# Splitting one of the two whole block products of a second channel matmul, with the residual moved into accumulating DMAs and the first load cut in quarters

## The chip, the cores and the metric

One core of a Trainium2 chip. The metric is the device time of one execution in microseconds (us). Profiles are single executions taken by the hardware profiler; their span is mostly 1.7 to 1.9 us shorter than the device time of the same execution. Ratios are computed as the mean time of one kernel's runs over that of the other kernel's runs of the same rounds, so they are not quite the ratio of the medians that are quoted.

## The reference, cut to what matters

```python
# attention with a hash mask, then an MLP mixer:
# x: (4, 768, 512), w_ch1: (512, 1536), w_ch2: (1536, 512), all fp32
u = x + h.transpose(0, 2, 1)                 # token mixing
h2 = np.maximum(u @ w_ch1, 0.0) @ w_ch2      # channel mixing: two matmuls
return (u + h2).astype(np.float32)           # "+ u" is the residual
```

The change touches the second channel matmul, the residual, and the first load of the attention.

## The kernel before: the parts that matter

Tokens are handled in three stages of 1024. In each, both channel matmuls are done by a Strassen-like scheme with seven block products instead of eight. In the second matmul five of the seven products, p2, p3, p5, p6 and p7, are themselves made of seven smaller ones (`product`); p1 and p4 are made whole (`whole_product`).

```python
def whole_product(s, j, name):               # 2 x 6 matmuls of 128x512
    ...
    for m in range(KC):
        accumulate(split(pair[:, m])[:, ns], lambda k: w[:, k, P*m:P*m+P],
                   lambda k: right[:, ns, k], range(HC))
    fetch_left(7 * s + j + 2)                # weights of the product after next

def product(s, j, name, q, between):         # 7 x 3 matmuls of 128x256
    part(0, 4, b00); part(1, 5, b10); ...    # small products into PSUM blocks
    for work in between: work()              # VectorE work of other blocks
    qs[:, 0] = ps[1] + p1; ...               # (VectorE) combine into q
    begin(ORDER[j + 1])                      # operand sums of the next product

ps = whole_product(s, 0, "p1")
...
product(s, 3, "p3", q3, [add(q57, q7, q5), residual(q57, 1, 1), residual(q7, 1, 0)])
product(s, 4, "p6", q6, [add(q3, q3, q5), residual(q3, 0, 1)])
product(s, 5, "p2", q2, [add(q6, q6, q1), add(q57, q57, q6), store(q57, 1, 1),
                         add(q3, q3, q6), store(q3, 0, 1), add(q7, q7, q6), residual(q1, 0, 0)])
ps = whole_product(s, 6, "p4")
add(q2, q2, q1)(); store(q2, 0, 0)()
for m in range(KC): ...                      # q7 += ps[m]; store in pieces
```

`residual` is a VectorE add of 128x1024; `store` a DMA of 512 KB from the SyncE queue. At the start, the first q and k come in two halves (each with both q and k), one on the SyncE and one on the ScalarE queue, while 14 dummy matmuls keep TensorE busy.

Of the kernel before, what the change touches and what calls it, by code (L numbers as in the profile page):

```python
# [48 lines left out]
def kernel(  # L49
# [214 lines left out]
    def attention(pool, psum, W1, W2, x0):  # L264
# [3 lines left out]
        def load_qk(n):  # L268
            if n >= len(pairs):
                return  # L270
            b, hp = pairs[n]
            t = pool.tile([P, 2, S], F32, name="qk", tag="qk", bufs=3)
            for sl in [slice(0, HALF), slice(HALF, S)] if n == 0 else [slice(0, S)]:
                issuer = nc.scalar if n == 0 and sl.start else nc.sync
                issuer.dma_start(out=t[:, :, sl], in_=qk[b, hp, :, :, sl])
            loaded[n] = [t, None, None, None]
# [171 lines left out]
        for _ in range(14):  # L448
            nc.tensor.matmul(idle[:D, :D], ones, ones, start=True, stop=True)
# [226 lines left out]
    def channels(pool, psum, SW1, second, TA, judge):  # L676
# [30 lines left out]
        def split(a):  # L707
            return a.rearrange("p (n t) -> p n t", n=2)

        def hidden(s, t):  # L710
# [18 lines left out]
            if s:  # L729
                look()  # L730
# [14 lines left out]
        ORDER = ["p1", "p5", "p7", "p3", "p6", "p2", "p4"]  # L745
        WHOLE = ["p1", "p4"]
# [3 lines left out]
        def prepare():  # L750
# [34 lines left out]
            return [[*sums, whole("p1"), whole("p4"), parts("p7")], *([parts(p)] for p in ["p3", "p6", "p5", "p2"])]  # L785
# [44 lines left out]
        def combine(to, a, op, b):  # L830
            for h in range(2):
                for n in range(2):
                    nc.vector.tensor_tensor(operand[to][h][n], operand[a][h][n], operand[b][h][n], op=op)

        def whole_product(s, j, name):
            pair = blocks()[2]
            if "WC2" in second:
                w = second.pop("WC2")[:, :HC, : DM // 2]
            else:
                w = left_at(7 * s + j)[:, : HC * 2 * P].rearrange("p (k c) -> p k c", k=HC)  # L840
            right = R[int(RIGHT[name][1])]
            for m in range(KC):
                final = s == last and name == ORDER[-1] and m == KC - 1
                for ns in [slice(0, 1), slice(1, 2)] if final else [slice(0, 2)]:
                    accumulate(
                        split(pair[:, m])[:, ns], lambda k: w[:, k, P * m : P * m + P],
                        lambda k: right[:, ns, k], range(HC),
                    )
            fetch_left(7 * s + j + 2)
            return pair  # L850

        def product(s, j, name, q, between):
# [26 lines left out]
            qs = q.rearrange("p i (n t) -> p (i n) t", n=2)  # L879
            nc.vector.tensor_tensor(qs[:, 0], ps[1], p1, op=ALU.add)  # L880
            nc.vector.tensor_tensor(p57[:, 0], p57[:, 0], p57[:, 1], op=ALU.add)
            if j + 1 < 6:
                begin(ORDER[j + 1])
# [5 lines left out]
        def outputs(s):  # L889
# [5 lines left out]
            def residual(to, i, n):  # L895
                return add(to, to, XT[:, KC * i : KC * i + KC, sl[n]])

            def store(q, i, n):
                return lambda: nc.sync.dma_start(
                    out=out[KC * i : KC * i + KC, :, sl[n]].rearrange("m p t -> p m t"), in_=q,  # L900
                )

            ps = whole_product(s, 0, "p1")
            combine("x", "r3", ALU.subtract, "r1")
            begin("p5")
            nc.scalar.copy(q1, ps)
            q7, q57, q3, q5 = [output_at(i) for i in range(4)]
            q6 = q2 = q5
            product(s, 1, "p5", q5, [lambda: combine("r0", "x", ALU.subtract, "r0")])
            product(s, 2, "p7", q7, [lambda: combine("r1", "r2", ALU.subtract, "x")])  # L910
            product(s, 3, "p3", q3, [add(q57, q7, q5), residual(q57, 1, 1), residual(q7, 1, 0)])
            product(s, 4, "p6", q6, [add(q3, q3, q5), residual(q3, 0, 1)])
            product(s, 5, "p2", q2, [
                add(q6, q6, q1), add(q57, q57, q6), store(q57, 1, 1), add(q3, q3, q6), store(q3, 0, 1),
                add(q7, q7, q6), residual(q1, 0, 0),
            ])
            ps = whole_product(s, 6, "p4")
            add(q2, q2, q1)()
            store(q2, 0, 0)()
            if s < last:  # L920
                inputs(s + 1, T, 0)
                inputs(s + 1, T, 1)
            for m in range(KC):
                final = s == last and m == KC - 1
                for cols in [slice(0, TT // 2), slice(TT // 2, TT)] if final else [slice(0, TT)]:
                    nc.vector.tensor_tensor(q7[:, m, cols], ps[:, m, cols], q7[:, m, cols], op=ALU.add)  # L926
                    issuer = nc.scalar if final and cols.start else nc.sync
                    at = slice(sl[0].start + cols.start, sl[0].start + cols.stop)
                    issuer.dma_start(out=out[KC + m, :, at], in_=q7[:, m, cols])
# [34 lines left out]
        for s in range(last + 1):  # L964
            for t in range(HC):
                if s == 0 and (t == 5 if judge else t == 0):
# [7 lines left out]
                else:  # L974
# [16 lines left out]
    def with_token_weights(stage):  # L991
        with tc.tile_pool(name="tok", bufs=1, reuse_waits="tile") as tok:
# [10 lines left out]
            f"p{i}": dram.tile([P, (4 if i in (1, 4) else 7) * n], F32, name=f"left{i}") for i in range(1, 8)  # L1003
# [95 lines left out]
```

## Time and profile before

| | |
|---|---|
| median of 4 runs, beside the changed kernel | 829.11 us (827.83 to 829.17) |
| medians of 9 to 11 runs in the three later sessions | 827.39 to 827.60 us |
| span of the profile | 825.5 us |
| TensorE busy | 816.4 us, 99% |
| VectorE busy | 630.3 us, 76% |
| the three channel stages, first to last matmul | 414.40 us |
| last matmul to end of span | 6.78 us |

Read a page from the engine shares and the chain that ended last: the chain tells which work set the end. Here it is one row of matmuls from the first load to the last store, so a change must be judged by what it does to TensorE's work, to the few microseconds before its first useful matmul and after its last, and to whether it is ever made to wait.

### The profile page before, as it was taken

To read this page: it belongs to the slowest core of one execution; us is meant where nothing else is said; L and a number is where in the kernel's file an instruction comes from. 1 tells how busy PE (TensorE), PEld (TensorE's weight loads), DVE (VectorE), ACT (ScalarE), POOL (GpSimd) and SP (SyncE) were. 2 spreads that over 40 slices of the span, in tenths; PEclk is the share of its full clock that TensorE was granted. 3 is DMA by queue.
4 is the path that set the end of the run, shared out by engine and by line. 5 is a ranking of instruction groups with operands and counts; after the bars stand their busy time and mean duration, and the time that the engine had idled before them with its cause. 6 is when DMAs were issued, how large, how long until landed. Compare 5 with 4: busy or idle time off the path is not lost.

```text
span 825.5 us, 9922 instructions
## 1 busy us (share of the span) xinstructions
PE 816.4 (99%) x3719; PEld 436.1 (53%) x3719; DVE 630.3 (76%) x831; ACT 326.0 (39%) x516; POOL 26.1 (3%) x37
## 2 busy tenths in 40 slices
PE   8999999999999999999999999999999999999996
PEld 4444444444444444455544468744447864444884
DVE  4889898989988667798486579956669984635993
ACT  5777788888887774211011211111111102121110
POOL 1000000000000000000011100001010001010000
PEclk9999999999999999999999999999999999999999
DMA  4335354546424226562014444453434345100432
GB/s 159 138 141 173 134 155 135 167 159 201 141 93 118 80 79 182 188 204 76 0 51 150 132 174 143 153 189 114 138 130 171 134 128 194 38 1 0 164 143 106
DMA packets 59784, 106.84 MB, mean 129 GB/s; under 512 B 28296, under 2 KB 37328, under 8 KB 57808
## 3 DMA queue, kind: packets, MB, share of 16 engines
q1 hardware_dynamic: 59168, 105.52, 38.7%
q8 instruction: 31, 0.51, 0.2%
q10 hardware_dynamic: 560, 0.61, 0.2%
q14 instruction: 25, 0.20, 0.1%
HBM read 84.43 MB, written 21.04 MB: 128 GB/s over the span
## 4 chain that ended last, share of the span: by engine, by line
PE 98%; DMA 0%; DVE 0%; ACT 0%; issue 0%; ACTq 0%
PE b L697 50%; PE sc L340 19%; PE acc L387 16%; PE t L618 5%; PE t L637 5%; PE sums L411 2%; PE hp L301 1%; DMA qk<-in_qk 0%; PE hw L319 0%; DVE second L926 0%; ACT vt L292 0%; ACT e L347 0%; ACT g L306 0%; DVE g L305 0%; DVE bits L321 0%
## 5 line engine op out<-in xcount | busy, mean ns | idle before, releaser
L704 ACT COPY p<-b 128x512 f32<-128x512 f32 (+1 forms) x84 | 44.3, 549 | 296.0 <-PE b L697 296.0
L340 PE MATMUL sc<-qk 64*128 64x384 f32 x768 | 158.5, 492 | 0.3 <-ACT e L347 0.3
L347 ACT ACTIVATE e<-sc 128x768 f32<-128x768 f32 x192 | 153.1, 812 | 13.4 <-PE sc L340 12.5
L697 PE MATMUL b<-R,second 128*128 128x256 f32 (+1 forms) x588 | 158.0, 427 | 0.0
L697 PEld LDWEIGHTS b<-R,second 128*128 128x128 f32 x588 | 111.7, 190 | 43.8 <-issue 32.0
L387 PE MATMUL acc<-e,vn 128*64 128x384 f32 x768 | 130.9, 490 | 0.0
L379 DVE TENSOR_TENSOR esd<-esd,e 128x768 f32<-128x768 f32 x128 | 122.3, 955 | 10.4 <-ACT e L347 0.5
L340 PEld LDWEIGHTS sc<-qk 64*128 64x128 f32 x768 | 66.5, 187 | 55.6 <-issue 45.1
L387 PEld LDWEIGHTS acc<-e,vn 128*64 128x64 f32 x768 | 52.3, 137 | 74.9 <-issue 74.3
L697 PE MATMUL b<-XT,WC 128*128 128x512 f32 x144 | 64.7, 592 | 0.0
L340 PE MATMUL sc<-bits 64*128 64x384 bf16 x384 | 62.9, 323 | 0.2 <-DVE bits L323 0.2
L731 POOL TENSOR_TENSOR p<-p,p 128x512 f32<-128x512 f32 x18 | 22.8, 1268 | 723.1 <-ACT p L704 723.1
L697 PEld LDWEIGHTS b<-XT,WC 128*128 128x128 f32 x144 | 27.3, 190 | 34.1 <-issue 33.6
L939 DVE TENSOR_REDUCE largest<-seen 128x1 f32<-128x1536 f32 x16 | 28.0, 1751 | 22.3 <-DMA seen<-in_qk 22.1
L618 PE MATMUL t<-x,W 128*128 128x512 f32 x96 | 41.8, 593 | 0.0
L736 DVE TENSOR_TENSOR R<-p,u 128x512 f32<-128x512 f32 x18 | 12.4, 687 | 38.5 <-POOL p L731 38.5
L637 PE MATMUL t<-W,r 128*128 128x384 f32 x128 | 41.8, 486 | 0.0
L736 DVE TENSOR_TENSOR R<-b,u 128x512 f32<-128x512 f32 x36 | 23.2, 686 | 24.1 <-PE b L697 24.1
L432 ACT COPY rec<-rec 32x384 f32<-32x384 f32 x64 | 32.6, 509 | 12.9 <-DVE rec L426 12.4
L375 DVE SCALAR_TENSOR_TENSOR esd<-e 128x768 f32<-128x768 f32 x32 | 30.5, 954 | 9.3 <-ACT e L347 9.3
L393 ACT ACTIVATE num<-acc,vsum 128x384 f32<-128x384 f32 x32 | 18.6, 581 | 41.6 <-PE acc L387 41.2
L697 PE MATMUL b<-TA,WC 128*128 128x512 f32 x72 | 33.8, 592 | 0.0
(116 smaller groups left out, 922.3 us busy)
## 6 DMA issues: line engine op xcount, KB each, us to landing
second<-left SPq DMA_DIRECT2D x15, 1344.0 KB
raw<-in_moe_w_ch SPq DMA_DIRECT2D x16, 768.0 KB
seen<-in_qk SPq DMA_DIRECT2D x16, 768.0 KB
qk<-in_qk SPq DMA_DIRECT2D x15, 768.0 KB
vn<-in_v SPq DMA_DIRECT2D x16, 384.0 KB
vt<-in_vT SPq DMA_DIRECT2D x16, 384.0 KB
bounced<-stage SPq DMA_DIRECT2D x32, 192.0 KB
x<-bounced SPq DMA_DIRECT2D x4, 1536.0 KB
```

What stands on the lines that cost most here:

```text
L340: nc.tensor.matmul(sc[:, i, :HALF], t[rows, 1, P * c : P * c + P], t[rows, 0, qs], start=start, stop=not start,)
L347: nc.scalar.activation(e, sc[:, :, :HALF], ACT.Exp, scale=SCALE)
L375: nc.vector.scalar_tensor_tensor(self.d, es[0], NR * EPS, es[1], op0=ALU.add, op1=ALU.add,)
L379: nc.vector.tensor_tensor(self.d, self.d, e, op=ALU.add)
L387: nc.tensor.matmul(acc[D * i : D * i + D], vn[:, i, c], e[:, i], start=(c == 0), stop=(c == NR - 1),)
L432: nc.scalar.copy(rec[other : other + 32, h], rec[at : at + 32, h])
L618: nc.tensor.matmul(ps, W1[:, r, P * j : P * j + P], x[:, r], start=(r == 0), stop=(r == NR - 1),)
L637: nc.tensor.matmul(ps[:, :HALF], r1[:, j, P * cb : P * cb + P], W2[:, j, HALF * half : HALF * half + HALF], start=(j == 0), stop=(j == NJ ...
L697: nc.tensor.matmul(ps, left(k), right(k), start=start and k == ks[0], stop=stop and k == ks[-1], skip_group_check=True,)
L704: nc.scalar.copy(c if shape is None else shape(c), ps)
L736: nc.vector.tensor_tensor(r[k], split(a), split(u), op=ALU.add)
L939: nc.vector.tensor_reduce(largest[:, n : n + 1], t, AX.XY, ALU.max, apply_absolute_value=True,)
```

## The change

The intent: p4 is split like the others, which saves an eighth of its matmul columns. To make room on VectorE, the residual adds go: the residual (XT) is written to the output early in each stage, and each finished block is added to it by an accumulating DMA, one per product. p6 and p3 trade places. The sums of weight blocks that a split needs come two per step instead of one. In the last stage q7 keeps its residual on VectorE and is stored plainly, in four pieces. The first load comes in two quarters and a half, with 16 dummy matmuls.

```diff
-            for sl in [slice(0, HALF), slice(HALF, S)] if n == 0 else [slice(0, S)]:
-                issuer = nc.scalar if n == 0 and sl.start else nc.sync
-                issuer.dma_start(out=t[:, :, sl], in_=qk[b, hp, :, :, sl])
+            if n:
+                nc.sync.dma_start(out=t, in_=qk[b, hp])
+            else:
+                for i in range(2):
+                    nc.sync.dma_start(out=t[:, i, :HALF], in_=qk[b, hp, :, i, :HALF])
+                nc.scalar.dma_start(out=t[:, :, HALF:], in_=qk[b, hp, :, :, HALF:])
...
-        for _ in range(14):
+        for _ in range(16):
...
-        ORDER = ["p1", "p5", "p7", "p3", "p6", "p2", "p4"]
-        WHOLE = ["p1", "p4"]
+        ORDER = ["p1", "p5", "p7", "p6", "p3", "p2", "p4"]
+        WHOLE = ["p1"]
...
             def store(q, i, n):
-                return lambda: nc.sync.dma_start(
-                    out=out[KC * i : KC * i + KC, :, sl[n]].rearrange("m p t -> p m t"), in_=q,
-                )
+                def job():
+                    nc.gpsimd.dma_start(
+                        out=out[KC * i : KC * i + KC, :, sl[n]].rearrange("m p t -> p m t"), in_=q,
+                        accum_op=ALU.add,
+                    )
+                return job
...
+            product(s, 3, "p6", q6, [add(q57, q7, q5)])
+            q3, q2, q4 = q6, q5, q57
+            product(s, 4, "p3", q3, [
+                add(q6, q6, q1), add(q57, q57, q6), store(q57, 1, 1), add(q5, q5, q6), add(q7, q7, q6),
             ])
-            ps = whole_product(s, 6, "p4")
+            end = [add(q3, q3, q5), store(q3, 0, 1)]
             if s < last:
+                product(s, 5, "p2", q2, end)
+                product(s, 6, "p4", q4, [
+                    add(q2, q2, q1), store(q2, 0, 0), lambda: inputs(s + 1, T, 0), lambda: inputs(s + 1, T, 1),
+                ])
+                add(q4, q4, q7)()
+                store(q4, 1, 0)()
+            else:
+                product(s, 5, "p2", q2, [*end, add(q7, q7, XT[:, KC:, sl[0]])])
+                product(s, 6, "p4", q7, [add(q2, q2, q1), store(q2, 0, 0)], ...)   # stores q7 plainly
...
+        def residual(s):                       # before the second step of each stage
+            ...  nc.sync.dma_start(out=out[...], in_=XT[...])
```

More of the change, by code (lines that the diff above doesn't have):

```diff
@@ L728, in hidden @@
             nc.vector.tensor_scalar(r[0], r[0], 0.0, None, op0=ALU.max)
-            if s:
+            if jobs:
+                for job in jobs.pop(0):
+                    job()
+            elif s:
                 look()
@@ L784, in prepare @@
             sums = weight_sums(WC2, SW2, slice(0, HC), slice(HC, NHT), low, high)
-            return [[*sums, whole("p1"), whole("p4"), parts("p7")], *([parts(p)] for p in ["p3", "p6", "p5", "p2"])]
+            return [
+                sums, [whole("p1"), parts("p7")], [parts("p6")], [parts("p3")], [parts("p5")], [parts("p2")],
+                [parts("p4")],
+            ]
         def place(i):
@@ L828, in begin, with combine @@
             nc.vector.tensor_tensor(b01, b01, b00, op=ALU.subtract)
-        def combine(to, a, op, b):
-            for h in range(2):
-                for n in range(2):
-                    nc.vector.tensor_tensor(operand[to][h][n], operand[a][h][n], operand[b][h][n], op=op)
+        def combine(to, a, op, b, where=[(0, 0), (0, 1), (1, 0), (1, 1)]):
+            for h, n in where:
+                nc.vector.tensor_tensor(operand[to][h][n], operand[a][h][n], operand[b][h][n], op=op)
         def whole_product(s, j, name):
@@ L842, in whole_product, with product @@
             for m in range(KC):
-                final = s == last and name == ORDER[-1] and m == KC - 1
-                for ns in [slice(0, 1), slice(1, 2)] if final else [slice(0, 2)]:
-                    accumulate(
-                        split(pair[:, m])[:, ns], lambda k: w[:, k, P * m : P * m + P],
-                        lambda k: right[:, ns, k], range(HC),
-                    )
+                accumulate(
+                    split(pair[:, m]), lambda k: w[:, k, P * m : P * m + P], lambda k: right[:, :, k], range(HC),
+                )
             fetch_left(7 * s + j + 2)
             return pair
-        def product(s, j, name, q, between):
+        def product(s, j, name, q, between, final=None):
             half = slice(0, TT // 2)
@@ L879, in product @@
             qs = q.rearrange("p i (n t) -> p (i n) t", n=2)
+            if final:
+                nc.vector.tensor_tensor(p1, p1, qs[:, 0], op=ALU.add)
             nc.vector.tensor_tensor(qs[:, 0], ps[1], p1, op=ALU.add)
+            if final:
+                nc.sync.dma_start(out=final(0, 0), in_=qs[:, 0])
             nc.vector.tensor_tensor(p57[:, 0], p57[:, 0], p57[:, 1], op=ALU.add)
-            if j + 1 < 6:
+            if final:
+                nc.vector.tensor_tensor(qs[:, 3], qs[:, 3], u, op=ALU.add)
+                nc.vector.tensor_tensor(qs[:, 3], qs[:, 3], p57[:, 0], op=ALU.add)
+                nc.sync.dma_start(out=final(1, 1), in_=qs[:, 3])
+                for i in (1, 2):
+                    nc.vector.tensor_tensor(qs[:, i], qs[:, i], u, op=ALU.add)
+                for i, a in [(1, ps[2]), (2, ps[3])]:
+                    nc.vector.tensor_tensor(qs[:, i], a, qs[:, i], op=ALU.add)
+                    (nc.scalar if i == 2 else nc.sync).dma_start(out=final(i // 2, i % 2), in_=qs[:, i])
+                return
+            if j < 6:
                 begin(ORDER[j + 1])
@@ L893, in add @@
                 return lambda: nc.vector.tensor_tensor(to, a, b, op=ALU.add)
-            def residual(to, i, n):
-                return add(to, to, XT[:, KC * i : KC * i + KC, sl[n]])
             def store(q, i, n):
-                return lambda: nc.sync.dma_start(
-                    out=out[KC * i : KC * i + KC, :, sl[n]].rearrange("m p t -> p m t"), in_=q,
-                )
+                def job():
+                    nc.gpsimd.dma_start(
+                        out=out[KC * i : KC * i + KC, :, sl[n]].rearrange("m p t -> p m t"), in_=q,
+                        accum_op=ALU.add,
+                    )
@@ L903, in outputs @@
+                return job
             ps = whole_product(s, 0, "p1")
-            combine("x", "r3", ALU.subtract, "r1")
+            combine("x", "r3", ALU.subtract, "r1", [(0, 1)])
             begin("p5")
+            combine("x", "r3", ALU.subtract, "r1", [(0, 0), (1, 0), (1, 1)])
             nc.scalar.copy(q1, ps)
-            q7, q57, q3, q5 = [output_at(i) for i in range(4)]
-            q6 = q2 = q5
+            q7, q57, q6, q5 = [output_at(i) for i in range(4)]
             product(s, 1, "p5", q5, [lambda: combine("r0", "x", ALU.subtract, "r0")])
@@ L910, in outputs @@
             product(s, 2, "p7", q7, [lambda: combine("r1", "r2", ALU.subtract, "x")])
-            product(s, 3, "p3", q3, [add(q57, q7, q5), residual(q57, 1, 1), residual(q7, 1, 0)])
-            product(s, 4, "p6", q6, [add(q3, q3, q5), residual(q3, 0, 1)])
-            product(s, 5, "p2", q2, [
-                add(q6, q6, q1), add(q57, q57, q6), store(q57, 1, 1), add(q3, q3, q6), store(q3, 0, 1),
-                add(q7, q7, q6), residual(q1, 0, 0),
-            ])
-            ps = whole_product(s, 6, "p4")
@@ L918, in outputs @@
-            add(q2, q2, q1)()
-            store(q2, 0, 0)()
+            product(s, 3, "p6", q6, [add(q57, q7, q5)])
+            q3, q2, q4 = q6, q5, q57
+            product(s, 4, "p3", q3, [
+                add(q6, q6, q1), add(q57, q57, q6), store(q57, 1, 1), add(q5, q5, q6), add(q7, q7, q6),
+            ])
+            end = [add(q3, q3, q5), store(q3, 0, 1)]
             if s < last:
-                inputs(s + 1, T, 0)
-                inputs(s + 1, T, 1)
-            for m in range(KC):
-                final = s == last and m == KC - 1
-                for cols in [slice(0, TT // 2), slice(TT // 2, TT)] if final else [slice(0, TT)]:
-                    nc.vector.tensor_tensor(q7[:, m, cols], ps[:, m, cols], q7[:, m, cols], op=ALU.add)
-                    issuer = nc.scalar if final and cols.start else nc.sync
-                    at = slice(sl[0].start + cols.start, sl[0].start + cols.stop)
-                    issuer.dma_start(out=out[KC + m, :, at], in_=q7[:, m, cols])
+                product(s, 5, "p2", q2, end)
[6 more added lines that the diff above has]
+                product(s, 5, "p2", q2, [*end, add(q7, q7, XT[:, KC:, sl[0]])])
+                product(s, 6, "p4", q7, [
+                    add(q2, q2, q1), store(q2, 0, 0),
+                ], lambda i, n: out[KC + i, :, sl[0].start + TT // 2 * n : sl[0].start + TT // 2 * (n + 1)])
@@ L932, in channels @@
+        def residual(s):
+            for i in range(2):
+                for n in range(2):
+                    if s < last or (i, n) != (1, 0):
+                        sl = slice(TT * (2 * s + n), TT * (2 * s + n) + TT)
+                        nc.sync.dma_start(
+                            out=out[KC * i : KC * i + KC, :, sl].rearrange("m p t -> p m t"),
+                            in_=XT[:, KC * i : KC * i + KC, sl],
+                        )
         unseen = list(range(len(pairs))) if judge else []
@@ L965, in channels @@
             for t in range(HC):
+                if t == 1:
+                    residual(s)
                 if s == 0 and (t == 5 if judge else t == 0):
@@ L973, in channels @@
                         job()
-                else:
+                elif (s, t) != (1, HC - 1):
                     look()
@@ L1002 @@
         "passed": {
-            f"p{i}": dram.tile([P, (4 if i in (1, 4) else 7) * n], F32, name=f"left{i}") for i in range(1, 8)
+            f"p{i}": dram.tile([P, (4 if i == 1 else 7) * n], F32, name=f"left{i}") for i in range(1, 8)
         }
```

## The prediction

> **What bounds the kernel now.** I read the page first (engine shares and the chain that ended last), then the TensorE timeline of the last stage, then that of VectorE, then the DMA share microsecond by microsecond.
>
> ```profile
> PE 816.4 (99%) x3719; PEld 436.1 (53%) x3719; DVE 630.3 (76%) x831; ACT 326.0 (39%) x516; POOL 26.1 (3%) x37
> ...
> PE 98%; DMA 0%; DVE 0%; ACT 0%; issue 0%; ACTq 0%
> ```
>
> TensorE (PE) works for 816.4 of 825.5 us and is 98% of the chain that ended last. So there are only three ways to save time: give PE less work, start it earlier, or shorten what follows its last matmul. PE must also never be made to wait. The work touched is the second channel matmul, done three times (once per stage of 1024 tokens) as seven block products p1 to p7. Before, p1 and p4 are made whole, the other five from seven smaller products each. The PE timeline of the last stage (start, duration, instructions):
>
> ```profile
> 752.58 14.35 PE L697 MATMUL b<-R,second 128*128 128x512 f32 x42
> 766.76 1.46 PE L697 MATMUL b<-second 128*128 128x256 f32 x6
> 768.05 7.93 PE L697 MATMUL b<-R,second 128*128 128x256 f32 x36
> 775.83 1.46 PE L697 MATMUL b<-second,second 128*128 128x256 f32 x6
> 777.12 7.93 PE L697 MATMUL b<-R,second 128*128 128x256 f32 x36
> 784.89 1.46 PE L697 MATMUL b<-second 128*128 128x256 f32 x6
> ...
> 799.13 4.05 PE L697 MATMUL b<-R,second 128*128 128x256 f32 x18
> 803.02 1.46 PE L697 MATMUL b<-second 128*128 128x256 f32 x6
> 804.32 14.38 PE L697 MATMUL b<-R,second 128*128 128x256 f32 x54
> ```
>
> An fp32 matmul appears as two instructions. A split product is 7 x 3 matmuls of 256 columns, 42 instructions. The marks 766.76, 775.83 and 784.89 (the fourth small product of three products in a row) lie 9.07 us apart: one split product takes **9.07 us**, 216 ns per instruction. A whole product is 12 matmuls of 512 columns, 24 instructions. The last p4 begins seven groups of 1.296 us after 799.13, at 808.2, and PE ends at 818.7; p1 runs from 752.58 to 762.9 (766.76 less three such groups). So it takes **10.3 us**, 429 ns per instruction.
>
> After the last matmul (VectorE and the issue queues):
>
> ```profile
> 818.73 1.35 DVE L926 TENSOR_TENSOR second<-b,second 128x512 f32<-128x512 f32 x3 [6.98 <-PE b L697]
> 819.45 0.96 SPq L929 DMA_DIRECT2D out<-second  x2
> 820.12 0.37 ACTq L929 DMA_DIRECT2D out<-second  x1
> ```
>
> VectorE sat idle for 6.98 us and only then did three adds: although half of p4's PSUM was finished 5 us before, its add waited for the last matmul. Then 512 KB leave at once. The DMA share shows data moving from 820.25 to about 822.1; the span ends 3.4 us after that.
>
> **What the Trainium skill says.** (1) "TensorE: Matmul & The Clock Gate", section "Wait — 56ns, not 53.3ns?": start to start is N / 2.4 GHz plus about 2.5 ns once warm. The trace has 429 and 216 ns per instruction for 512 and 256 columns, twice what that gives (431 and 218), with a granted clock of 1.00; the ratio is 1.99, so halving the width costs nothing visible. (2) "DMA: Bandwidth & Descriptors", section "SWDGE vs HWDGE vs iDMA": accumulation during a DMA is done only by DMAs issued from GpSimd. The kernel before has none, so no row shows their cost. (3) Same page, "Anatomy of one DMA — SWDGE (gpsimd) path": about 2.0 us plus bytes / 436e3; for 512 KB that is 3.2 us for a plain copy. (4) Same page, "Rules for kernel authors": an accumulating DMA reads its destination and writes it later, so it must wait for the earlier DMA. The early residual write and the later addition are therefore ordered by a semaphore; the trace before cannot show that wait.
>
> **The change part by part.**
>
> *p4 split.* Removed per stage: 24 x 429 ns = 10.30 us of PE; added: 42 x 216 ns = 9.07 us. The gain is 1.23 us a stage, **3.7 us** for three, all on the path, if PE stays fed. Weight loads do not take over: 42 x 190 ns = 8.0 us, beside 9.07.
>
> *VectorE.* Removed per stage: four residual adds of 1.22 us (three in the last stage) and p4's two 0.69 us adds, 6.3 us. Added: p4's operand sums (4 x 0.95), its four combinations (3 x 0.42 + 0.69) and the addition of q7 (1.22), 7.0 us. So the total hardly moves (+0.7 us), but its place does. The tightest spot by program order is p3, now fifth: two operand sums, four adds (4.9 us), two small adds, then the two sums that p2's operand needs. Placing them by durations before, relative to p3's start: operand sums done at 3.7 us, adds at 8.6, small adds at 9.2, p2's operands at 11.2. PE wants p2's third group at 9.07 + 2.59 = 11.66. That leaves a half microsecond of slack: I expect no stall or one of a few tenths.
>
> *DMA.* These rows of the windows (stretch, its length, busy time of PE, weight loads, VectorE, ScalarE and GpSimd, granted clock, then DMA share and GB/s) show what a weight fetch costs:
>
> ```profile
> 772.00:773.00 1.00, 1.00 (x6) 0.89 (x5) 1.00 (x3) 0.00 (x0) 0.00 (x0) 1.00 0.00 0
> 773.00:774.00 1.00, 1.00 (x6) 0.88 (x5) 1.00 (x2) 0.37 (x1) 0.00 (x0) 1.00 1.06 226
> 774.00:775.00 1.00, 1.00 (x7) 0.87 (x6) 0.70 (x2) 0.00 (x0) 0.00 (x0) 1.00 0.99 409
> 775.00:776.00 1.00, 1.00 (x6) 0.90 (x5) 1.00 (x2) 0.00 (x0) 0.00 (x0) 1.00 0.99 419
> 776.00:777.00 1.00, 1.00 (x6) 0.87 (x6) 1.00 (x2) 0.00 (x0) 0.00 (x0) 1.00 0.77 323
> ```
>
> Issued when a product's matmuls end (771.9), 1344 KB are there by about 777; the product that needs them starts at 781.0. p4's fetch grows from 768 to 1344 KB, like the others. An accumulating store of 512 KB moves at most 1 MB through HBM, an estimate of 2.6 us at 400 GB/s, less than those 4 us of slack. The early residual is 2 MB a stage, about 5 us at that rate, in the matmul phase, where the queue is half idle. Its worst effect is in the first stage: six weight-sum jobs now come two per step of 12.05 us, share one buffer, and queue behind the 2 MB. I estimate that VectorE falls behind by some 7 us there, but PSUM and the copies are buffered two steps deep, so PE should not stop.
>
> *Start.* PE's first useful matmul starts at 4.92 us, 0.81 us after the warm-up matmuls end, waiting for the first 384 KB, which travel interleaved with 384 KB from the other queue. A first part half as large is there after some 470 of 780 KB, which at the rates of the first microseconds (about 390 GB/s by then) is some 0.7 us earlier; with two more warm-up matmuls (0.11 us each) ending at 4.3, I count **0.5 us**.
>
> *Tail.* Now the last adds are two of 256 columns (0.77 us instead of 1.38, if both wait for the last matmul), and 256 KB instead of 512 are stored at the end: 0.8 us from issue to first data as before, about 0.6 us instead of 1.6 moving. PE end to last data: 2.2 instead of 3.35 us, **1.1 us** gained.
>
> Sum: 3.7 + 0.5 + 1.1 = 5.3 us. I subtract an expected 0.5 us for small stalls and for the chance that the accumulation ends last: 829.1 - 4.8 = **824.3 us**, 0.6% less.
>
> **Rivals.**
> (a) *The last accumulating store sets the end.* It is issued after q2 is complete, about 5.3 us into p4, and must land within 9.07 - 5.3 + 2.2 = 6.0 us to be hidden. The skill's 3.2 us plus a second read fits; an accumulate at half rate with slow descriptor making on GpSimd does not. One in three; it would cost 1 to 4 us, giving 825 to 828.
> (b) *VectorE becomes the bound inside the products.* For: it is 90 to 100% busy in those windows and p3's slack is half a microsecond. Against: the operand sums come a product ahead. A stall of 0.3 to 1 us in each stage would give 825 to 827.
> (c) *DMA backlog stalls PE in the first stage*, through the shared weight-sum buffer behind the residual. For: two sums a step, against one before. Against: rates near 400 GB/s, and some 5 us of margin even when VectorE is 7 us late. If it happened, 2 to 6 us lost, giving 826 to 830.
> (d) *Accumulating DMAs are much slower than assumed* and delay the weight fetches of every stage: several us each, 830 to 845. Unlikely, 4%.
>
> **Range and chances.** Without any stall 823.8, a little below that if the tail is better; with (a) or (b) up to 828. So 822.0 to 827.8. Two per cent is 16.6 us: no gain here adds up to that, and a loss needs (d) in every stage. Faster by over 2%: 0.01; within: 0.96; slower: 0.03.
>
> **What would show it.** The PE timeline should show p4 as groups of 128x256 and the stage's seven products taking 10.3 + 6 x 9.07 us. PE idle inside the stages should stay under 1 us; idle laid to VectorE in p2 would be (b), to DMA (d), in the first stage's steps (c). The first useful matmul should start at about 4.4 us. After the last matmul there should be two 256-column adds and data for about 2.2 us; if DMA data run on longer, or the chain ends in the GpSimd queue's store, it is (a). The prediction is wrong if PE's idle time grows by more than about 4 us anywhere.

## The result, and the profile after

The changed kernel took 824.48 us (median of 4 runs, 823.69 to 825.05) beside 829.11 us for the kernel before: 4.6 us less; the ratio of the means is 0.9947 (95% interval 0.993 to 0.9964). 824.3 us had been predicted. Two later sessions on other chips gave 824.10 beside 827.55 us (ratio 0.9955) and 824.32 beside 827.60 us (0.9953), which is 3.3 to 3.9 us by one measure or the other. The changed kernel is where it was predicted; the kernel before had in the first session mostly runs of its slower sort, to which I come back.

The TensorE timeline of the changed kernel's last stage (start, duration, engine and line, operation, tiles, shape, instructions):

```profile
751.45 14.35 PE L700 MATMUL b<-R,second 128*128 128x512 f32 x42
765.64 1.46 PE L700 MATMUL b<-second 128*128 128x256 f32 x6
...
801.90 1.46 PE L700 MATMUL b<-second 128*128 128x256 f32 x6
803.19 7.93 PE L700 MATMUL b<-R,second 128*128 128x256 f32 x36
810.96 1.46 PE L700 MATMUL b<-second,second 128*128 128x256 f32 x6
812.26 4.05 PE L700 MATMUL b<-R,second 128*128 128x256 f32 x18
```

The last product now has 256-column groups, and the marks 801.90 and 810.96 show p2 and p4 at a distance of 9.06 us. The chain that ended last shows the same over all stages. Before, its two pieces of channel matmuls (start, duration) are:

```profile
404.48 336.13 PE b L697 x992
740.61 0.11 PE b L955
740.72 77.99 PE b L697 x298
```

and after:

```profile
405.82 333.66 PE b L700 x1028
739.49 0.11 PE b L990
739.60 76.72 PE b L700 x304
```

Each is unbroken: 414.23 against 410.49 us, so **3.74 us** less. But the second starts 1.34 us later than the first: in this pair of profiles the start lost time. The TensorE timeline of the start, before (in brackets the idle time just before and what ended it):

```profile
4.92 1.53 PE L319 MATMUL hw<-qk,projs 128*128 128x384 f32 x4 [0.81 <-DMA qk<-in_qk]
...
9.01 0.91 PE L319 MATMUL hw<-qk,projs 128*128 128x384 f32 x2
```

and of the changed kernel:

```profile
4.61 2.46 PE L322 MATMUL hw<-qk,projs 128*128 128x384 f32 x4
7.00 2.21 PE L343 MATMUL sc<-qk 64*128 64x384 f32 x12
9.04 0.65 PE L343 MATMUL sc<-bits 64*128 64x384 bf16 x6
10.35 0.91 PE L322 MATMUL hw<-qk,projs 128*128 128x384 f32 x2 [0.66 <-DMA qk<-in_qk]
```

The first useful matmul is earlier, 4.61 instead of 4.92 us, but the same four instructions take 2.46 us instead of 1.53, and at 10.35 us TensorE had waited for the other half of the load. The trace's record of the granted clock explains the first: full clock from 6.45 us on, against 3.83 us in the profile of before.

The end, on all engines:

```profile
812.37 1.21 POOL L921 DMA_DIRECT2D out<-second  x1 [6.66 <-DVE p L889]
...
816.34 0.76 DVE L901 TENSOR_TENSOR second<-b,second 128x256 f32<-128x256 f32 x2 [0.59 <-PE b L700]
816.79 0.33 SPq L902 DMA_DIRECT2D out<-second  x1
817.13 0.37 ACTq L902 DMA_DIRECT2D out<-second  x1
```

Two adds of 256 columns after the last matmul, as predicted. But GpSimd issued the last accumulating store at 812.37 us, and the DMA view gives such stores (last number: median us from issue to landing)

```profile
out<-second POOLq DMA_DIRECT2D x11, 512.0 KB, 6.0
```

so it was still under way beside the final plain stores: its last data moved at 818.2 us, and it landed at 818.6. The last data of the final stores themselves moved 3.7 us after the last matmul, against 3.3 us in the profile of before and 2.2 us in the prediction. From the last matmul (816.32) to the end of the span (822.92) are 6.60 us, only 0.2 less than before.

### The profile page after: what moved, and what is told of

Read it like the earlier page. It is cut to its first block, busy times and chain, and to the rows that moved or that the text cites. A ratio compares the mean times of both kernels' runs of the same rounds, so it can differ in the third digit from the quotient of the medians.

```text
span 822.9 us, 10100 instructions
## 1 busy us (share of the span) xinstructions
PE 814.2 (99%) x3765; PEld 445.1 (54%) x3765; DVE 637.8 (78%) x848; ACT 330.0 (40%) x525; POOL 39.8 (5%) x48
## 4 chain that ended last, share of the span: by engine, by line
PE 97%; DMA 1%; ACT 0%; DVE 0%; issue 0%; ACTq 0%
PE b L700 50%; PE sc L343 19%; PE acc L390 16%; PE t L621 5%; PE t L640 5%; PE sums L414 2%; PE hp L304 1%; DMA qk<-in_qk 1%; PE hw L322 0%; ACT vt L295 0%; ACT e L350 0%; ACT g L309 0%; DVE g L308 0%; DVE bits L324 0%; DVE second L901 0%
## 5 line engine op out<-in xcount | busy, mean ns | idle before, releaser
L707 ACT COPY p<-b 128x512 f32<-128x512 f32 (+1 forms) x90 | 47.2, 545 | 296.7 <-PE b L700 292.1
L700 PE MATMUL b<-R,second 128*128 128x256 f32 (+1 forms) x612 | 150.9, 404 | 0.0
L700 PEld LDWEIGHTS b<-R,second 128*128 128x128 f32 x612 | 116.3, 190 | 32.5 <-issue 18.4
L640 PEld LDWEIGHTS t<-W,r 128*128 128x128 f32 x128 | 24.3, 190 | 17.6 <-issue 1.4
```

The lines of the kernel that those rows point to most:

```text
L640: nc.tensor.matmul(ps[:, :HALF], r1[:, j, P * cb : P * cb + P], W2[:, j, HALF * half : HALF * half + HALF], start=(j == 0), stop=(j == NJ ...
L700: nc.tensor.matmul(ps, left(k), right(k), start=start and k == ks[0], stop=stop and k == ks[-1], skip_group_check=True,)
L707: nc.scalar.copy(c if shape is None else shape(c), ps)
```

## The experiments

Twelve kernels ran in three sessions, each on another chip, with five rounds each and the kernel before in the same rounds. All gave correct results. For each, the profile was cut at three places: the first channel matmul, the last matmul, and the end of the span. "Full clock" is the time, from the span's start, at which the trace first records the granted TensorE clock at 1 (the expectation of `again` counts these times 0.25 us later: 6.70 and 4.08).

| kernel | full clock, us | channel starts, us | channel length, us | last matmul to end, us | span, us | median, us | before, same rounds |
|---|---|---|---|---|---|---|---|
| before | 3.83 | 404.31 | 414.40 | 6.78 | 825.49 | 829.11 | |
| changed | 6.45 | 405.66 | 410.66 | 6.60 | 822.92 | 824.48 | 829.11 |
| again (the same) | 3.87 | 403.96 | 410.65 | 6.38 | 820.99 | 824.10 | 827.55 |
| again2 (the same) | 5.82 | 405.72 | 410.66 | 6.61 | 822.99 | 824.32 | 827.60 |
| s1 (changed, old start) | 10.24 | 407.00 | 410.66 | 6.66 | 824.32 | 824.08 | 827.55 |
| s2 (before, new start) | 4.48 | 403.99 | 414.40 | 7.01 | 825.40 | 827.25 | 827.55 |
| s3 (before, 18 dummies) | 4.01 | 404.45 | 414.40 | 6.66 | 825.51 | 827.37 | 827.55 |
| t1 (last accumulation gone) | 6.85 | 405.22 | 410.65 | 6.37 | 822.24 | 822.89 | 827.39 |
| t2 (t1, own PSUM tile) | 4.42 (lost again, 11.24 to 14.66) | 407.41 | 411.71 | 5.98 | 825.10 | 823.01 | 827.39 |
| a1 (split, no accumulation) | 6.41 | 404.92 | 410.66 | 5.81 | 821.39 | 823.35 | 827.39 |
| a2 (accumulation, no split) | 8.96 | 406.28 | 414.97 | 9.78 | 831.03 | 832.13 | 827.39 |
| a0 (a1, old start) | 4.30 | 404.33 | 410.66 | 6.55 | 821.54 | 823.32 | 827.60 |
| b1 (a1, own PSUM tile) | 4.38 | 404.30 | 410.66 | 6.02 | 820.98 | 822.61 | 827.60 |
| b2 (b1, one queue at start) | 5.14 | 404.28 | 410.65 | 5.76 | 820.69 | 822.56 | 827.60 |

The channel length hardly scatters: 414.40 in all three kernels with a whole p4 and plain stores, 410.65 or 410.66 in nine of the ten profiles with a split one. The start scatters by 3.5 us, mostly with the clock. The latest start, that of t2, is another matter: there TensorE waited 2.08 us for the second half of the first load, and then lost the full clock again for 3.4 us.

### again: the changed kernel a second time

No edit.

> The changed kernel unaltered, for its spread and a second profile. Two things at its start are open: in the first profile the granted TensorE clock became full at 6.70 us (4.08 us in the profile of before), and the second half of the first load, on the ScalarE queue, landed only at 10.3 us. If the late clock is chance (a matter of phase), it should lie elsewhere here; if the change causes it, near 6.7 us again. If the straggling load is caused by cutting the first load in quarters, its last bytes land after 8 us again. Time expected 824 to 825 us, 4 to 5 us under before.

Measured: 824.10 us, ratio 0.9955 (0.9942 to 0.9968). The full clock came at 3.87 us this time, so its time in the first profile was not made by the change. The straggling load is the change's: the second half of the first load landed at 7.6 to 10.8 us in all eight profiles with quarters and that half on the ScalarE queue, and at 6.6 to 7.2 us in the five with the old start. TensorE waited for it in five of the eight: 0.66 us in the first profile, 0.17 here, 1.04 in again2, 0.28 in b1, and most in t2:

```profile
10.80 1.25 PE L322 MATMUL hw<-qk,projs 128*128 128x384 f32 x2 [2.08 <-DMA qk<-in_qk]
```

With the clock at the same time as in the profile of before, the channel part starts 0.35 us earlier than there.

### s1, s2, s3: the start alone

```diff
 s1, on the changed kernel: quarters -> halves again, range(16) -> range(14)
 s2, on the kernel before:  halves -> quarters,       range(14) -> range(16)
 s3, on the kernel before:                            range(14) -> range(18)
```

s1:

> The changed kernel with its start undone: first load in halves, 14 warm-up matmuls; split p4 and accumulating stores stay. Theory A (the start gained about 0.5 us on average): 824.8 to 825.3 us. Theory B (the start is worth about 1 us or more, because closing the TensorE gap before the first useful matmul lets the clock become full sooner in most runs): 825.5 to 826.5. Theory C (the start lost, as the two profiles taken alone suggest, 1.3 us): 823.0 to 823.7.

s2:

> The kernel before with the new start alone: first load in quarters, 16 warm-up matmuls. Theory A: 0.5 us faster than before (828.5). Theory B: 1 to 2 us faster (827 to 828). Theory C: about 1 us slower (830).

s3:

> The kernel before with 18 instead of 14 warm-up matmuls and the load left as it was: the TensorE gap of 0.8 us before the first useful matmul is filled, the data come no earlier. Theory A (earlier data are the gain): same as before or 0.1 us slower. Theory B (the gap delays the full clock): 1 us or more faster than before.

Measured: s1 824.08 us (again: 824.10); s2 827.25 us, ratio to before 0.9999 (0.9986 to 1.0012); s3 827.37 us, ratio 0.9998 (0.9985 to 1.001). None of the three theories is resolved in the times: B's gain of 1 us or more and C's loss of 1 us lie at or beyond the edges of s2's interval, which is 1.1 us either way, and A's 0.5 us lies within it, as does nothing at all. The profile of s1 shows what else the start can do:

```profile
5.14 2.90 PE L319 MATMUL hw<-qk,projs 128*128 128x384 f32 x4 [0.88 <-DMA qk<-in_qk]
7.96 3.31 PE L340 MATMUL sc<-qk 64*128 64x384 f32 x12
```

After a gap of 0.88 us the full clock came only at 10.24 us: the twelve score instructions took 3.31 us instead of 2.21, and the channel part started 2.7 us later than in the profile of before.

The Trainium skill, "TensorE: Matmul & The Clock Gate", section "What's actually happening", says that the clock is released after at least one busy window of about 3.4 us, and that this window is free-running, not tied to the kernel's start. The traces agree: the stretches of full clock that they record are whole multiples of 3.413 us (819.20 us is 240 of them, 812.37 us is 238). They also show how busy is busy enough here. Counted from the matmul records, TensorE was busy for 2.83 to 3.41 us of the window before the release in all fourteen profiles, and for at most 2.75 us (a2; s1: 2.53) of any earlier window. So with a gap it depends on where the windows fall: in the four profiles with 14 dummies and a gap the full clock came at 3.83, 4.30, 8.96 and 10.24 us, never in between; in the ten where dummies and data follow each other more closely, it came between 3.87 and 6.85.

In the times no effect on the average shows: runs over 1.5 us above the fastest of their kernel and session are 9 of 53 with the old start (the kernel before, s1, s3, a2 and a0 in the later sessions) and 6 of 38 with the new one (again, s2, t1, t2, a1, again2, b1). What the new start is worth on average remains open within about a microsecond.

### t1: the last accumulating store made plain

```diff
-  product(s, 5, "p2", q2, [*end, add(q7, q7, XT[:, KC:, sl[0]])])
+  product(s, 5, "p2", q2, [*end, add(q7, q7, XT[:, KC:, sl[0]]), add(q1, q1, XT[:, :KC, sl[0]])])
   product(s, 6, "p4", q7, [
-      add(q2, q2, q1), store(q2, 0, 0),
+      add(q2, q2, q1), lambda: nc.sync.dma_start(out=out[:KC, :, sl[0]]..., in_=q2),
...  # and the early residual write of that block left out
```

> The changed kernel with one store less accumulated: in the last stage q2's residual is added by VectorE (to q1, in p2) and q2 is stored plainly. Theory D (the last accumulating store, 6.0 us from issue to landing, shares the DMA engines with the final stores and eats the tail gain): last matmul to last data falls from 3.8 to 4.0 us to about 2.2, and the time by 1 to 1.5 us against the changed kernel, 822.6 to 823.2 on this chip's scale of 824.1. Theory E (the end has a fixed length that the stores do not set): data end earlier, time the same within 0.3 us.

Measured: 822.89 us, ratio 0.9945 (0.9932 to 0.9959). In another session the changed kernel itself had 0.9955, so the intervals overlap. The last matmul to the end is 6.37 us, against 6.38 to 6.66 in the four profiles with that store (changed, again, again2, s1). If that is D's direction, the size is far less than expected. Of the final stores all but 28 KB had moved by 2.2 us after the last matmul, as D says (in the changed kernel 130 KB were then still to come); but those 28 KB, nearly all on the ScalarE queue, straggled until 3.9 us.

### t2: one small block of the last product in its own PSUM tile

```diff
+  if final:
+      ps[3] = psum.tile([P, TT], F32, name="b0", tag="b0", bufs=2)[:, half]
...  # and the copy of both blocks made in two pieces
```

> As t1, and one of the last product's four small blocks gets a PSUM tile of its own, so that the addition of the other block need not wait for the last matmul. Under D: VectorE ends 0.4 us after the last matmul instead of 0.8, 128 KB instead of 256 KB leave after it, another 0.4 to 0.7 us off: 822.0 to 822.8. Under E: as t1.

Measured: 823.01 us (822.16 to 826.71), ratio 0.9941 (0.9927 to 0.9954). The last add ended 0.45 us after the last matmul instead of 0.78, and the end fell to 5.98 us. But this profile, of the slowest of its six runs (826.71 us), is also the one with the late start (2.08 us of waiting for the first load, above) and with a longer channel part, 411.71 us. The TensorE timeline of the second stage:

```profile
668.04 4.05 PE L700 MATMUL b<-R,second 128*128 128x256 f32 x18
672.88 4.15 PE L700 MATMUL b<-R,second 128*128 128x256 f32 x18 [0.79 <-DMA second<-left]
```

p4 waited for its weights. Their fetch had been issued at 663.05 us and landed 9.78 us later; the accumulating store of q57 had been issued just before it, at 660.35. t2 does not change that stage, so this is something the changed kernel can meet as well. The traces show how near it is: fetches follow one another every 9.07 us, but in every profile of the changed kernel the data of p4's fetch begin some 1.2 us late (800.3 us in the last stage, where 799.1 was due), while the store is still moving. Without accumulation (a1) they begin on time. The margin differs less. p4's fetch has 9.07 us; from issue to landing it took 6.5 to 7.9 us in 17 of the 18 cases with accumulation (six profiles of three stages), 9.78 in the one shown, and 6.6 to 6.8 us in the twelve cases without (a1, a0, b1, b2).

### a1: the split without accumulation and without early residual

```diff
   def job():
-      nc.gpsimd.dma_start(out=..., in_=q, accum_op=ALU.add)
+      nc.sync.dma_start(out=..., in_=q)
...
-  product(s, 3, "p6", q6, [add(q57, q7, q5)])
+  product(s, 3, "p6", q6, [add(q57, q7, q5), residual(q57, 1, 1), residual(q7, 1, 0)])
...
-  end = [add(q3, q3, q5), store(q3, 0, 1)]
+  end = [add(q3, q3, q5), residual(q3, 0, 1), store(q3, 0, 1), residual(q1, 0, 0)]
...
-  if t == 1: residual(s)           # the early write
```

> The changed kernel with p4 split but the residual added by VectorE again and all stores plain (no accumulation, no early residual). Theory F (the residual had to leave VectorE, because the split fills it): TensorE is kept waiting for p2's and p4's operand sums, 0.3 to 1 us a stage, and the channel part is 411.5 to 413.5 us long instead of 410.7. Theory G (VectorE has room enough, the accumulation buys nothing): 410.7 us, and the time is 1 us below the changed kernel, since the end has no accumulating store.

Measured: 823.35 us (822.8 to 823.5), ratio 0.9949 (0.9935 to 0.9963). Its chain that ended last has the same two unbroken pieces as the changed kernel's:

```profile
405.08 333.66 PE b L700 x1028
...
738.86 76.72 PE b L700 x304
```

Theory G holds for the channel part: TensorE never waited. The residual did not have to leave VectorE. The VectorE timeline of the last stage shows by how little (the sums that p2 needs; p2 began at 797.45 us, so its third group was due at 800.04):

```profile
797.40 0.95 DVE L836 TENSOR_TENSOR second<-R 128x768 f32<-128x768 f32 x1
798.39 0.96 DVE L837 TENSOR_TENSOR R<-R 128x768 f32<-128x768 f32 x1
```

They end at 799.35, 0.7 us ahead. The same sums in the changed kernel end at 800.08, due at 800.78: 0.7 us too. The two adds fewer in p6 bought nothing: at the turn from p6 to p3 VectorE waited 1.6 us for TensorE in the changed kernel and 0.25 us in a1. The expected full microsecond at the end came in this profile (5.81 us against 6.78), but not in that of a0 (6.55), which has the same end. That a1 is 1 us faster than the changed kernel, as G says, is not shown: its ratio of 0.9949 lies within the intervals of the changed kernel's in the other sessions (0.9955, 0.9953).

### a2: the accumulation without the split

```diff
 on the kernel before: store() and, in the first two stages, p4's stores accumulate
 from the GpSimd queue; XT is written early; residual adds removed (q7 of the last stage keeps its own)
```

> The kernel before with p4 still whole, its residual put in the output early and blocks added by DMA (p4's row blocks of the first two stages too). Both theories: the channel part stays 414.4 us long and the time that of before within 0.4 us, because VectorE is not on the path there; last accumulating store issued some 7 us before the last matmul, so not at the end. If accumulating DMAs slow the weight fetches, the channel part grows by over 1 us.

Measured: 832.13 us, ratio 1.0052 (1.0038 to 1.0066): 4.3 us slower. Neither theory had this. The GpSimd timeline of its first stage:

```profile
531.41 1.33 POOL L899 DMA_DIRECT2D out<-second  x1 [55.47 <-DVE second L893]
538.24 1.23 POOL L899 DMA_DIRECT2D out<-second  x1 [5.49 <-DVE TA L581]
544.52 1.21 POOL L899 DMA_DIRECT2D out<-second  x1 [5.05 <-issue]
545.50 1.16 POOL L931 DMA_DIRECT2D out<-second  x1
553.97 0.89 POOL L931 DMA_DIRECT2D out<-second  x1 [7.30 <-ACT u L704]
554.55 1.59 POOL L731 TENSOR_TENSOR p<-p,p 128x512 f32<-128x512 f32 x1
```

q57 and q3 are ready almost together here, as in the kernel before, but their stores begin 6.8 us apart and the next 6.3 us after, about the 6 us that one takes to land. In all three stages each later store of 512 KB was issued 0.3 us after the one before it had landed (here 537.98 and 544.26 us), while one of 256 KB (545.50) was issued with a larger one still under way. The kernel makes none of these first-stage stores wait for the one before it; they wait for the residual write and for VectorE's sum of the block (the releasers in brackets are inferred from the times of events, and L581 and L704 are not among what these stores wait for). In the last stage the three stores are issued at 808.23, 814.71 and 820.87 us, so the last one begins about when the last matmul ends (821.25) and moves until 827.3: the end is 9.78 us long instead of 6.78, and that is most of the loss. In the first stage the GpSimd add of the next stage (L731) stood in line behind the stores until 554.55 us; the chain that ended last leads from there to the one gap of TensorE in the channel part, 0.34 us at 629.79 us. Spacing them "one block per product" in the changed kernel is what keeps this out of sight. Which resource makes them follow one another is not settled; only that it is not a wait in the program.

### again2, a0, b1, b2: together on one chip

again2, the changed kernel:

> The changed kernel a third time, as the measure for the three beside it. Channel part 410.7 us; as in both its profiles, the weight fetch in flight beside an accumulating store should begin 1 us later than the others and end with less margin. About 3.5 us under before.

a0, a1 with the old start:

> The split of p4 alone (with the order of products that goes with it): first load in halves, 14 warm-up matmuls, residual by VectorE, plain stores. If the split is the whole gain: channel part 410.7 us (3.74 us less), last matmul to end of span 5.8 us (1 us less than before), together 4.7 us under before, and not slower than the changed kernel.

b1, a1 with t2's PSUM tile:

> As a1 (split, residual by VectorE, plain stores, new start), and one of the last product's small blocks in a PSUM tile of its own, so that the addition of the other need not wait for the last matmul. Last VectorE add 0.4 us after the last matmul instead of 0.8; 0.3 to 0.6 us below a1, that is 4.5 to 5 us under before. If the end is set by something other than the stores, as a1 within 0.2 us.

b2, on b1:

```diff
-  nc.scalar.dma_start(out=t[:, :, HALF:], in_=qk[b, hp, :, :, HALF:])
+  nc.sync.dma_start(out=t[:, :, HALF:], in_=qk[b, hp, :, :, HALF:])
```

> As b1, with the second half of the first load issued on the same queue as the quarters, behind them, instead of the ScalarE queue. If the straggling bytes of that half (landing at 8 to 10 us in the profiles of the changed kernel) come from sharing the engines with the other queue's later loads, they land by 6 us and no matmul waits for them, and the first quarter lands about 0.3 us earlier: first useful matmul 4.2 us instead of 4.6, 0.3 to 0.7 us below b1.

Measured, beside 827.60 us for before: again2 824.32 us (0.9953; 0.994 to 0.9966), a0 823.32 us (0.9951; 0.9937 to 0.9965), b1 822.61 us (0.9939; 0.9926 to 0.9952), b2 822.56 us (0.9935; 0.9923 to 0.9948). a0 is the split of p4 almost alone, and it has all that the changed kernel has: 410.66 us of channel part, and a time that is not higher. b1 and b2 are **the fastest kernels**; all six runs of b2 (822.15 to 823.02) lie below all six of again2 (823.13 to 824.77). b2's chief aim is met: the second half of the load landed at 6.69 us (8.95 in b1), and no matmul waits for it:

```profile
4.60 1.81 PE L322 MATMUL hw<-qk,projs 128*128 128x384 f32 x4
6.34 2.21 PE L343 MATMUL sc<-qk 64*128 64x384 f32 x12
8.38 0.65 PE L343 MATMUL sc<-bits 64*128 64x384 bf16 x6
8.96 0.91 PE L322 MATMUL hw<-qk,projs 128*128 128x384 f32 x2
```

The first useful matmul did not come earlier, though: the 16 dummies end just then, and the first quarters landed at 4.07 us, hardly before the 4.12 us of b1. Against b1 nothing is resolved in the time.

## Why the prediction was right or wrong

**p4 split: right, and nearly all of the gain.** 3.7 us predicted, 3.74 measured, in every profile where nothing stalled. That TensorE stays fed held in the channel part of nine of the ten profiles with a split p4; the other is t2 (1.06 us lost). a2, without the split, lost 0.57 us where the accumulating stores crowd.

**VectorE: right.** Predicted slack before p2 half a microsecond, measured 0.7. Rival (b) fell: a1 puts three to four more adds per stage on VectorE and loses nothing. What the prediction did not ask is whether the residual had to move at all. It did not.

**DMA: the mechanism right, one term too small.** The accumulating store of 512 KB was put at 2.6 us of DMA time; its data move for about 4 us (814.2 to 818.2 us for the last one of the changed kernel), from issue to landing it takes 6.0 us, and while it runs the windows show a poor yield (length, busy times of PE, weight loads, VectorE, ScalarE and GpSimd, granted clock, DMA share, GB/s; changed kernel, end):

```profile
814.00:815.00 1.00, 1.00 (x6) 0.90 (x5) 0.77 (x2) 0.17 (x1) 0.00 (x0) 1.00 1.07 96
815.00:816.00 1.00, 1.00 (x7) 0.80 (x5) 0.76 (x3) 0.00 (x0) 0.00 (x0) 1.00 1.03 145
816.00:817.00 1.00, 0.30 (x2) 0.00 (x0) 0.66 (x2) 0.00 (x0) 0.00 (x0) 1.00 1.03 190
```

The DMA engines are busy all the time and yet move 96 to 190 GB/s, against 409 in the weight fetch shown in the prediction (the bytes counted there may leave out what an accumulation reads). The prediction gave the weight fetch 4 us of slack. p4's fetch had 1.2 to 2.6 us, and once, in t2, nothing; but without accumulation it had only 2.2 to 2.5 us. So accumulation explains half a microsecond of the shrinkage at the median (7.2 against 6.7 us to landing) and the one stall. Rival (d) was the right worry at a smaller size.

**First-stage backlog (c): right that it would be harmless.** The waits of the changed kernel show VectorE waiting four times for the shared buffer (total, times, longest):

```profile
DVE seen L779 <- DMA left<-seen: 11.0, 4, 4.0
```

and TensorE's piece of 333.66 us has no gap.

**Start: 0.5 us predicted, not confirmed.** The step that failed is not "A first part half as large is there ... some 0.7 us earlier": the quarters landed by 4.06 to 4.22 us, the halves before by 4.78 to 5.00. It is that this was taken as a gain in time, and first of all "two more warm-up matmuls (0.11 us each) ending at 4.3". Each dummy appears as two instructions of 0.107 us while the clock is low, so two more cost 0.43 us; in all new-start profiles but one they ended at 4.6 to 4.7 us, and TensorE took up the data only then. The first useful matmul is 0.3 to 0.6 us earlier than in the profile of before, but its worth is 0.35 us in one pair of profiles in which the clock came alike (before and again), nothing in another (a0 and b1), and nothing measurable in s2. The prediction had overlooked two more things: when the full clock is granted moves the start by up to 3 us between profiles, and the half on the ScalarE queue lands later when the quarters and the next loads go out on the other queue (up to 2.08 us of waiting, in t2).

**Tail: 1.1 us predicted, 0.3 measured.** Means of the profiles: 6.82 us for the kernels with the old end (before, s2, s3), 6.56 with the changed end (changed, again, again2, s1), 6.24 without an accumulating store at the end (t1, a0, a1) and 5.92 where the PSUM tile comes to that (t2, b1, b2). The step that failed is "PE end to last data: 2.2 instead of 3.35 us": the last data moved 3.6 to 3.8 us after the last matmul with the changed end. Rival (a), put at one in three, may be part of it: the last accumulating store's data ran on until 1.9 us after the last matmul, sharing the engines with the final stores. By the means it is worth 0.3 us, but the single values overlap (5.81 to 6.55 without it, 6.38 to 6.66 with it). The other part is the straggling end of the final stores, 3.9 to 4.1 us after the last matmul even without that store, which the estimate of "about 0.6 us moving" did not contain.

**The sum** thus agreed better than its parts. 3.7 + 0.5 + 1.1 - 0.5 was predicted; 3.7 + about 0.3 of tail + at most 0.4 of start is what the profiles hold. That is near the 3.3 to 3.9 us of the later sessions. That the time itself was met to 0.2 us is luck in part: 4.8 us were taken off a kernel before at 829.1 us; taken off its 827.6 us of two later sessions they would have given 822.8, where 824.1 and 824.3 were measured. The 4.6 us of the first session come with a kernel before whose median was 829.11 us there and 827.4 to 827.6 in three later sessions; the late full clock shown by s1 is the size of such a difference, but no profile of those runs exists, so this is argued, not shown.

## What to carry to other kernels

Where TensorE is 98% of the chain, count matmul columns: that term came out to 0.04 us, and no other gain in the sum came out near its estimate. Before moving work off an engine that looks full, check by a run without the move whether the engine is ever waited for: the accumulating DMAs that came with this split paid for nothing, took 6 us each and cost some slack in p4's weight fetch. Differences of a microsecond at the start of a kernel need several profiles, because the granted clock alone moves them by up to three.

## What the Trainium skill lacked or had wrong

- "DMA: Bandwidth & Descriptors", section "Anatomy of one DMA — SWDGE (gpsimd) path", gives about 2.0 us plus bytes / 436e3, by which I estimate 3.2 us for 512 KB. The accumulating stores of 512 KB from SBUF into HBM took 5.8 to 6.2 us from issue to landing (medians in the profiles of the changed kernel, again, t1 and a2). No page gives a time for such an accumulating store; how much of it is the accumulation and how much the GpSimd path is not shown, since no run stores plainly from GpSimd.
- The same page says who must issue such a DMA and what must be waited for, but not that several in a row follow one another: in a2 those of 512 KB were issued 6.1 to 6.8 us apart, each 0.3 us after the one before had landed, although the program set no wait between those of the first stage, and GpSimd's other work stood behind them (L731 at 554.55 us).
- The same page, section "Issuing engines are not separate DMA queues", says that DMAs of different engines interleave on the same 16 engines. It lacks that a small load can end very late through that: 384 KB on the ScalarE queue, issued at 1.20 us, landed at 10.3 us in the profile of the changed kernel, beside larger loads on the SyncE queue, and at 6.7 us in b2, where it went out on that queue itself.
- "TensorE: Matmul & The Clock Gate" does not say how busy its window must be: here 2.83 of 3.41 us was enough for the full clock and 2.75 us was not, and one window with 1.34 us (t2, the wait of 2.08 us) lost it again for 3.41 us, where one with 2.21 us (again2) did not.
